# A recurrence and an MLP on one core: transposes moved to the DMA crossbar, relu and copies split over two engines, a new order of issue

## The chip, the cores and the metric

The kernel runs on one core of a Trainium2 chip. A core has a matrix engine (TensorE, PE in the profile; its weight loads are listed as PEld), two elementwise engines that can read the matrix results in PSUM (VectorE, DVE, and ScalarE, ACT), a third one that works from SBUF (GpSimd, POOL), and a queue engine (SyncE, SP) that in this kernel issues every DMA. Each engine runs its own list of instructions in order and waits on semaphores where its data or its buffer come from another. The metric is the device time of one execution in microseconds (us), median of several.

## The reference

Four sequences of 768 tokens with 8 heads of 48 columns go through a decaying recurrence, and its output through a two-layer MLP:

```python
# r, k, v, w: (4, 8, 768, 48) float32, u: (8, 48)
for t in range(S):
    cur = einsum('bhd,bhe->bhde', u[None] * kt, vt)
    y[:, :, t] = einsum('bhd,bhde->bhe', rt, state + cur)
    state = wt[:, :, :, None] * state + einsum('bhd,bhe->bhde', kt, vt)
x = y.transpose(0, 2, 1, 3).reshape(3072, 384)
h = x @ w_in                     # 384 -> 2048
g = s * relu(h) ** 2 + b
out = g @ w_out                  # 2048 -> 384, float32
```

## The kernel before

The recurrence is cut into 24 chunks of 128 tokens (the first two are packed from halves). Inside a chunk the decays become exponentials of running sums of log w, and the rest is matmuls. Two chunks make one of 12 token pairs (T), which go through the MLP. A plan names every step, and the string `ORDER` lists them in the order in which they are written to the engines' queues. `n` is a chunk, `T.i` a step of a token pair, `+18` means 18 matmuls on zeros [...], and `@A`, `@D`, `@P` move one step to ScalarE, VectorE or GpSimd.

- `load n.0 ... n.3`: w, r, k, v of a chunk, 192 KB each (384 KB where packed). `li`, `lo`: a quarter of w_in, w_out (768 KB); `ci`, `co`: its cast to bf16.
- `ln`, `cum` (TensorE: running sums, one PSUM buffer A, shared with `mt`), `exp`, from chunk 8 also `inc`, `exn`: the decay factors. `mul` (VectorE): r and k times these.
- `tr`, `tev`: r and k transposed, by TensorE and a ScalarE copy, or by one crossbar DMA (then only `tev`).
- `mt`, `msk`: scores and their mask. `ymm`, `yev`: output y, with `yd` added, the part of u (`rkp`, `rku`, `cd`, `yd`). `dmm`, `sup`, `st`: state. `vb`: cast of v.
- `xtr`, `xev`: y transposed into x for the MLP, by TensorE and a copy, or by one crossbar DMA.
- `g1` (h = x w_in, 6 matmuls, two PSUM buffers h), `relu`, `sq`, `g2` (out, 4 matmuls), `oev`, `store`.
- `colsum`, `cssplit`, `csspread`, `csevac`: the constant b times the column sums of w_out. `u_mm`, `u_ev`: u spread over 128 partitions by a matmul, and its copy to SBUF.

```python
    def xbar_rk(n):
        return n >= DTK or (n >= DK2 and n % 2 == 1)      # DTK = 9: r and k by crossbar from chunk 9
    def xbar_x(n):
        return n >= DTX or (n >= DX2 and n % 2 == 1)      # DTX = 24: x never
# ...
    def trans(n):                                          # tr: 8 matmuls
        ps = psB.tile([128, 8, 128], BF16, name="trps", tag="B")
        for x in range(2):
            for p in range(HP):
                nc.tensor.matmul(ps[:, x * HP + p, :], lhsT=c["prd"][...], rhs=identity,
                    is_transpose=True, ...)
    def dtrans(n):                                         # tev by crossbar
        RK = work.tile([128, 2 * HP, 128], BF16, name="RK", tag="RK", bufs=RKB)
        nc.sync.dma_start_transpose(out=RK, in_=c["prd"].rearrange("t x h d -> t (x h d)"))
    def dxtr(n):                                           # xev by crossbar
        nc.sync.dma_start_transpose(out=xT[T][:, :, j * L : (j + 1) * L], in_=cb[n]["x"])
    def xtr(n):                                            # 3 matmuls
        for i in range(KT):
            nc.tensor.matmul(ps[:, i, :], lhsT=c["x"][:, i * 128 : (i + 1) * 128], rhs=identity, ...)
    def xevac(n):
        nc.scalar.copy(out=xT[T][:, :, j * L : (j + 1) * L], in_=c["xt_ps"])
    def relu(T, i):
        rh = mlp.tile([128, FPQ, TOK], BF16, name="rh", tag="rh", bufs=4)
        nc.scalar.activation(out=rh, in_=hs[T, i], func=AF.Relu)
    def square(T, i):
        if pl.ops["sq", T, i]["eng"] == "ACT":
            nc.scalar.activation(out=g, in_=rh, func=AF.Square)
        else:
            nc.vector.tensor_tensor(out=g, in0=rh, in1=rh, op=ALU.mult)
# ...
    def spread_u():
        ps = psO.tile([128, HD], FP32, name="u_ps", tag="o")
        nc.tensor.matmul(ps, lhsT=one_row, rhs=u_row, start=True, stop=True)
    def u_evac():
        nc.vector.tensor_copy(out=u_bc, in_=os_.pop("u"))
```

Of the kernel before, what the change touches and what calls it, by code (L numbers as in the profile page):

```python
# [24 lines left out]
PK = 2  # L25
PKD = 1.55
ONE = 8
DTK = 9
DTX = 24
DK2 = 24  # L30
DX2 = 24
SQE = 'DA'
# [15 lines left out]
g11.3 load6.0 colsum1 rkp4 g20.1 ln5 relu1.2 tr4 rku4 relu1.3 load4.3 cum5 sq1.0@A g11.4 st1 exp5
g11.5 co2 g20.5 tev4 load5.1 sq1.3 load5.2 colsum2 sq1.1@A st3 co3 mt4 load7.0 relu1.4 g20.6
relu1.5 cd4 g11.6 load6.1 msk4 sq1.5@A colsum3 ln6 g20.7 yd4 sq1.4@A load6.2 cssplit g11.7 sq1.2@A  # L50
l25 l24 vb4@A csspread load5.3 cum6 csevac g20.2 mul5 exp6 load8.0 dmm4 g20.3 rkp5 sup4 ln7
load6.3 tr5 oev0.0 ymm4 rku5 tev5 cum7 load7.1 yev4 g21.0 oev0.1 exp7 l26 xtr4 mul6 load7.2 g21.1
xev4 mt5 relu1.6 cd5 vb5 load7.3 g21.4 relu1.7 st2 msk5 yd5 dmm5 g21.2 ln8 load9.0 sq1.7@A st4
sup5 tr6 cum8 vb6 store0.1 tev6 ymm5 rkp6 g21.5 yev5 exp8 load8.1 g21.6 inc8 l27 sq1.6@A dmm6 xtr5
mul7 g21.7 load8.3 xev5 exn8 mt6 rkp7 sup6 vb7@A load8.2 g12.0 msk6 load9.1 g12.1 rku7 ln9 tr7
oev1.1 relu2.0 load10.0 rku6 cum9 relu2.1 cd7 dmm7 g12.2 inc9 tev7 l28 load11.0 g12.3 cd6 st5
relu2.2 ymm6 yd6 sup7 load9.2 exp9 g12.4 relu2.3 sq2.0 mt7 yd7 yev6 exn9 load9.3 g12.5 relu2.4
msk7 st7 g21.3 sq2.2@A store0.0 sq2.1 rkp8 g12.6 oev1.0 sq2.3 load10.1 ymm7 relu2.6 st6 xtr6 g22.4
yev7 ln10 load10.2 mul8 relu2.5 g22.0 ln11 xtr7 sq2.4 load12.0 g22.5 xev6 sq2.6@A load10.3 cum10
vb9 g12.7 xev7 inc10 vb8 exp10 tr8 load11.1 sq2.5@D relu2.7 g22.1 l29 mul9 exn10 g13.0 load11.2  # L60
tev8 rku8 cum11 g22.6 load12.1 relu3.0 dmm9 rkp9 exp11 cd8 g13.1 sq2.7 tev9 sup9 dmm8 g13.2 rku9
relu3.1 inc11 sq3.0@A g22.2 mul10 relu3.2 load13.0 g13.3 exn11 load11.3 rkp10 sup8 mt8 relu3.3
g13.4 msk8 ln12 tev10 vb10 g22.7 sq3.2@A st9 sq3.1 g13.5 oev2.1 relu3.4 yd8 cum12 store1.0 ymm8
relu3.5 inc12 g22.3 l210 yev8 exp12 store1.1 g13.6 cd9 sq3.4@A mul11 sq3.3 xtr8 dmm10 mt9 load15.0
g23.0 yd9 msk9 vb11@A g13.7 st8 xev8 load14.0 g23.1 oev2.0 relu3.6 l212 rku10 sup10 load12.2 exn12
ymm9 g23.4 sq3.5 load12.3 yev9 relu3.7 rkp11 mt10 cd10 xtr9 tev11 g23.2 msk10 xev9 l211 rku11 ln13
g23.5 g14.0 sq3.6 load13.1 sq3.7@D cum13 load13.2 relu4.0 dmm11 g14.1 inc13 exp13 mul12 ymm10
exn13 load14.1 g14.2 ln14 l213 cd11 relu4.1 yd10 g23.6 relu4.2 cum14 sq4.0 load13.3 g14.3 exp14
yd11 sup11 g23.3 inc14 relu4.3 load16.0 st11 g14.4 sq4.1 oev3.0 st10 mt11 load14.2 yev10 relu4.4
g14.5 msk11 rkp12 sq4.2@A xtr10 load15.1 sq4.3 g14.6 vb12 ln15 g23.7 rkp13 relu4.6 load15.2 ymm11  # L70
relu4.5 cum15 yev11 rku12 g24.0 xev10 tev12 oev3.1 g14.7 ln16 mul13 xtr11 exn14 g24.4 store2.1
# [12 lines left out]
inc19 exp19 load19.1 g16.7 mul18 load19.2 g17.0 relu6.7 tev16 g26.1 exn19 ln20 dmm16 g26.5 vb18@A
sup16 load19.3 sq6.7 cum20 g17.1 vb17 inc20 relu7.0 tev17 g26.6 rkp18 sq6.6@A dmm17 relu7.1 g17.2
st16 exp20 load20.1 dmm18 g26.7 sq7.0@A mul19 exn20 g26.2 tev18 relu7.2 rkp17 oev6.1 g17.3 sup17
mt16 rku17 relu7.3 load20.2 g17.4 msk16 sq7.3 g26.3 yd16 relu7.4 load21.0 g17.5 sup18 sq7.2@A vb19
cd17 sq7.1 ymm16 rku18 tev19 oev6.0 mt17 relu7.5 g27.0 msk17 l219 yd17 g27.4 st17 load21.1 g17.6
yev16 ymm17 st18 load21.2 xtr16 mt18 yev17 xev16 g27.5 sq7.5@D relu7.6 load22.0 sq7.4 xtr17 cd18
g17.7 xev17 mul20 ln21 g27.1 relu7.7 dmm19 load20.3 yd18 msk18 g18.0 sq7.7 sq7.6@A g27.2 rkp19  # L90
store5.1 sup19 relu8.0 g27.6 rku19 mt19 tev20 g18.1 msk19 rkp21 ymm18 relu8.1 g18.2 load23.0 sq8.0
g27.3 store6.1 rku21 cd19 relu8.2 load22.1 cum21 ln22 g18.3 sq8.1@D exp21 ymm19 yd19 inc21 relu8.3
g18.4 oev7.0 sq8.2@A rkp20 g27.7 load22.2 yev19 relu8.4 yev18 g18.5 sq8.3 rku20 oev7.1 load23.1
mt20 relu8.5 load21.3 xtr18 xtr19 msk20 vb20@A g18.6 xev18 g28.0 load22.3 relu8.6 supn20 sq8.5@D
g18.7 sq8.4 xev19 store6.0 exn21 cum22 g19.0 relu8.7 inc22 rkp22 ln23 g28.1 load23.2 relu9.0 g28.4
mul21 sq8.6@A store7.0 g19.1 exp22 supn21 cd20 exn22 g28.5 tev21 yd20 relu9.1 cum23 ymm20 exp23
g19.2 yev20 g28.6 inc23 relu9.2 mul22 g19.3 sq8.7 exn23 g28.2 tev22 sq9.1 mul23 g19.4 sq9.2@A
xtr20 relu9.3 cd21 g28.3 load23.3 sq9.0 sq9.3 g28.7 yd21 oev8.0 relu9.4 store7.1 g19.5 store8.0
rku22 mt21 relu9.5 g19.6 vb22 msk21 sq9.5 st19 g29.4 vb21@A tev23 xev20 g19.7 oev8.1 relu9.6
supn22 cd22 ymm21 sq9.4@A g29.5 yd22 yev21 relu9.7 mt22 sq9.6@A vb23 g29.0 sq9.7@D xtr21 rkp23  # L100
msk22 g29.6 xev21 g29.1 rku23 g110.0 ymm22 relu10.0 g110.1 yev22 mt23 cd23 relu10.1 g110.2 yd23
msk23 xtr22 g29.7 relu10.2 supn23 sq10.0@A g110.3 xev22 ymm23 relu10.3 g110.4 yev23 g29.2 sq10.1@D
relu10.4 g110.5 sq10.3 sq10.4 oev9.1 xtr23 g110.6 relu10.5 sq10.2 xev23 g210.0 sq10.5@D relu10.6
g110.7 g111.0 relu10.7 g210.1 relu11.0 g111.1 g210.2 relu11.1 g111.2 sq11.0@A sq10.6@A g29.3
sq10.7 g111.3 oev9.0 relu11.2 g210.3 sq11.1@D relu11.3 store9.0 store8.1 g111.4 sq11.2@A g210.4
relu11.4 g111.5 g210.5 relu11.5 g111.6 sq11.5@D oev10.0 g210.6 relu11.6 sq11.3@D store10.0 g111.7
store9.1 g211.0 relu11.7 g210.7 sq11.4@A sq11.7@D sq11.6@A g211.1 oev10.1 g211.4 store10.1 g211.2
g211.8 g211.5 g211.3 g211.6 oev11.0 g211.9 g211.7 store11.0 g211.10 oev11.1 g211.11 store11.1
oev11.2 store11.2
"""  # L110

class Plan:

# [43 lines left out]
def kernel(  # L160
# [550 lines left out]
        T, j = divmod(n, CPT)  # L711
        if j == 0:
            xT[T] = mlp.tile([128, KT, TOK], BF16, name="xT", tag="xT", bufs=XTB)
        nc.scalar.copy(out=xT[T][:, :, j * L : (j + 1) * L], in_=c["xt_ps"])  # L714


    def load_win(i):
# [40 lines left out]

    def relu(T, i):
        rh = mlp.tile([128, FPQ, TOK], BF16, name="rh", tag="rh", bufs=4)  # L760
        nc.scalar.activation(out=rh, in_=hs[T, i], func=AF.Relu)  # L761
        hs[T, i] = rh

    def sq_eng(T, i):
# [385 lines left out]
```

## Time and profile before

| | |
|---|---|
| time, median of 3 (range) | 187.29 us (186.79 to 187.95) |
| profiled span | 186.2 us |
| granted TensorE clock | 0.999 |
| relu on ScalarE | 96 x 598 ns |
| square on ScalarE, on VectorE | 62 x 629 ns, 34 x 482 ns |
| x transposes: matmuls, copies | 72 x 219 ns, 24 x 478 ns |
| r and k transposes: matmuls, copies | 72 x 219 ns, 9 x 1013 ns |
| r and k transposes by crossbar | 15, landing in 3.3 us (2.7 to 5.2) |
| mask on VectorE | 24 x 1220 ns |
| bytes read, written | 25.17 MB, 4.72 MB |

A mean duration is that of one instruction from its start to its end; on TensorE and ScalarE neighbours overlap, so a sum of durations is more than the engine's busy time. In the profile PEq, SPq and DVEq are the engines' sequencers, L748 is a line of the kernel (h), L792 the out matmuls, L297 the loads, L477 the r and k transposes by TensorE, L451 and L444 `mul`, L532 the first `mt`.

### The profile page before, as it was taken

What the parts mean: (1) busy time and instruction counts of PE and PEld (TensorE: products, weight loads), DVE (VectorE), ACT (ScalarE), POOL (GpSimd) and SP (SyncE); (2) the same over time, 40 slices, a digit from 0 to 9 for tenths busy, and PEclk for the clock granted to TensorE, in tenths of its full rate; (3) what the DMA queues carried; (4) which work ended last, traced back from release to release, by engine and by line L of the source; (5) the groups of instructions that cost most, each with busy time, mean ns of one, the idle gap of its engine ahead of it and who ended that gap; (6) DMA issues with size and microseconds to landing.
All of it is one profiled execution on the core that took longest, in us unless ns stands there. A gap on an engine that the chain in (4) does not pass through costs nothing.

```text
span 186.2 us, 5073 instructions
## 1 busy us (share of the span) xinstructions
PE 180.6 (97%) x1994; PEld 142.3 (76%) x1994; DVE 131.5 (71%) x220; ACT 142.4 (76%) x277; POOL 103.8 (56%) x141
## 2 busy tenths in 40 slices
PE   7999999999999999999999999999999999999992
PEld 5667888866678788687778877877787877887871
DVE  7478888556799768986987878658788577452231
ACT  3576798797979999769798779974689886678530
POOL 3787840608798695949956265695892167100000
PEclk9999999999999999999999999999999999999999
DMA  6998999888989999999488989999698272000322
GB/s 161 264 308 239 331 318 280 295 180 177 207 190 229 197 221 240 187 213 188 118 199 171 246 164 252 194 186 208 146 212 211 59 184 59 2 0 4 112 99 86
DMA packets 117610, 34.14 MB, mean 183 GB/s; under 512 B 112338, under 2 KB 115539, under 8 KB 117587
## 3 DMA queue, kind: packets, MB, share of 16 engines
q1 hardware_dynamic: 117586, 33.83, 78.3%
q8 instruction: 15, 0.25, 0.5%
q14 instruction: 9, 0.07, 0.1%
HBM read 25.17 MB, written 4.72 MB: 160 GB/s over the span
## 4 chain that ended last, share of the span: by engine, by line
PE 74%; SPq 12%; DMA 7%; DVE 4%; issue 1%; DVEq 0%
PE o_ps L792 31%; PE h_ps L748 29%; SPq L297 8%; DMA wi_st<-in_moe_w_in_dram 5%; PE mt_ps L543 3%; DMA rkt<-in_k_dram 2%; PE y_ps L606 2%; PE xt_ps L699 2%; PE y_ps L597 2%; PE cums L388 2%; PE d_ps L638 1%; DVE gT L773 1%; SPq L719 1%; SPq L305 1%; PE trps L477 1%; SPq L729 1%
## 5 line engine op out<-in xcount | busy, mean ns | idle before, releaser
L748 PE MATMUL h_ps<-xT,w_in 128*128 128x256 bf16 x576 | 77.6, 273 | 0.1
L792 PE MATMUL o_ps<-w_out,gT 128*128 128x384 bf16 (+1 forms) x400 | 75.3, 320 | 0.0
L761 ACT ACTIVATE rh<-h_ps 128x512 bf16<-128x512 f32 x96 | 56.5, 598 | 14.5 <-PE h_ps L748 13.5
L748 PEld LDWEIGHTS <-w_in 128*128 128x128 bf16 x576 | 60.6, 114 | 6.7 <-POOL w_in L880 0.2
L792 PEld LDWEIGHTS <-gT 128*128 128x128 bf16 x400 | 36.2, 98 | 15.3
L771 ACT ACTIVATE gT<-rh 128x512 bf16<-128x512 bf16 x62 | 37.2, 629 | 0.3
L352 POOL TENSOR_TENSOR yd<-vt,cd 128x384 bf16<-128x384 f32 x22 | 20.1, 919 | 30.4 <-DVE cd L346 18.3
L554 DVE TENSOR_TENSOR mt_sb<-mt_ps,tri_strict 128x1024 bf16<-128x1024 f32 x22 | 26.8, 1219 | 4.2 <-PE mt_ps L543 3.8
L323 POOL TENSOR_TENSOR rkp<-rkt 128x384 f32<-128x384 f32 x22 | 24.5, 1112 | 4.7 <-DMA rkt<-in_k_dram 4.6
L329 POOL TENSOR_TENSOR rku<-rkp,u_bc 128x384 f32<-128x384 f32 x24 | 26.0, 1087 | 0.9
L451 DVE TENSOR_TENSOR prd<-rkt,E 128x768 bf16<-128x768 f32 x22 | 23.0, 1045 | 2.8 <-DMA rkt<-in_k_dram 1.6
L803 DVE SCALAR_TENSOR_TENSOR o_sb<-o_ps,s_bc,bconst 128x384 f32<-128x384 f32 (+1 forms) x25 | 14.9, 596 | 10.3 <-PE o_ps L792 10.0
L651 DVE TENSOR_TENSOR x_sb<-y_ps,yd 128x384 bf16<-128x384 f32 x24 | 13.2, 554 | 11.3 <-PE y_ps L606 10.4
L773 DVE TENSOR_TENSOR gT<-rh 128x512 bf16<-128x512 bf16 x34 | 15.8, 482 | 4.9 <-ACT rh L761 4.9
L714 ACT COPY xT<-xt_ps 128x384 bf16<-128x384 bf16 x24 | 11.5, 478 | 6.8 <-PE xt_ps L699 6.8
L346 DVE TENSOR_REDUCE cd<-rku 128x8 f32<-128x384 f32 x24 | 13.0, 543 | 0.9 <-POOL rku L329 0.9
L688 POOL TENSOR_TENSOR st<-stmp,l 128x384 bf16<-128x384 bf16 x16 | 13.1, 829 | 0.7 <-DVE stmp L679 0.7
L1109 PE MATMUL warm_ps<-warm_sb 128*128 128x256 bf16 x74 | 12.2, 309 | 1.1 <-DVE warm_sb L1066 1.1
L424 DVE TENSOR_TENSOR inc<-cums,logw 128x384 f32<-128x384 f32 x16 | 8.9, 554 | 5.5 <-ACT rh L761 1.6
L318 ACT ACTIVATE logw<-wt 128x384 bf16<-128x384 f32 x22 | 11.5, 522 | 1.5 <-DMA wt<-in_w_dram 1.3
L880 POOL CAST vb<-vt 128x384 bf16<-128x384 f32 x14 | 7.4, 536 | 7.6 <-DMA vt<-in_v_dram 4.9
L464 POOL TENSOR_TENSOR l<-E,par 128x8 f32<-128x8 f32 x20 | 7.0, 353 | 6.6 <-ACT E L419 4.7
(96 smaller groups left out, 198.1 us busy)
## 6 DMA issues: line engine op xcount, KB each, us to landing
out_dram<-o_sb SPq DMA_DIRECT2D x23, 192.0 KB, 2.8
wt<-in_w_dram SPq DMA_DIRECT2D x22, 192.0 KB, 3.9
rkt<-in_r_dram SPq DMA_DIRECT2D x22, 192.0 KB, 4.0
rkt<-in_k_dram SPq DMA_DIRECT2D x22, 192.0 KB, 3.8
vt<-in_v_dram SPq DMA_DIRECT2D x22, 192.0 KB, 3.7
wi_st<-in_moe_w_in_dram SPq DMA_DIRECT2D x4, 768.0 KB, 7.5
wo_st<-in_moe_w_out_dram SPq DMA_DIRECT2D x4, 768.0 KB, 7.6
pkt<-in_w_dram SPq DMA_DIRECT2D x1, 384.0 KB, 3.3
```

What stands on the lines that cost most here:

```text
L297: nc.sync.dma_start(out=dst, in_=src[bb, :, t0 : t0 + L, :].transpose([1, 0, 2]))
L323: nc.gpsimd.tensor_tensor(out=rkp, in0=c["r"], in1=c["k"], op=ALU.mult)
L329: nc.gpsimd.tensor_tensor(out=rku.rearrange("t h d -> t (h d)"), in0=c["rkp"].rearrange("t h d -> t (h d)"), in1=u_bc, op=ALU.mult,)
L352: nc.gpsimd.tensor_tensor(out=yd, in0=c["v"], in1=c["cd"].unsqueeze(2).to_broadcast([128, H, D]), op=ALU.mult,)
L451: nc.vector.tensor_tensor(out=prd[:, :, :, 0:D], in0=c["rk"], in1=c["E"][:, :, 0:HD].rearrange("t x (h d) -> t x h d", h=H), op=ALU.mult,)
L554: nc.vector.tensor_tensor(out=m.rearrange("s g p t -> s (g p) t"), in0=c["mt_ps"].rearrange("s g p t -> s (g p) t"), in1=(masks[n % 2] if ...
L748: nc.tensor.matmul(ps[:, f, :], lhsT=w_in_sb[ft // FPP][:, kt, :].rearrange("p (m j) -> p j m", j=FPP)[:, ft % FPP, :], rhs=xT[T][:, kt, : ...
L761: nc.scalar.activation(out=rh, in_=hs[T, i], func=AF.Relu)
L771: nc.scalar.activation(out=g, in_=rh, func=AF.Square)
L773: nc.vector.tensor_tensor(out=g, in0=rh, in1=rh, op=ALU.mult)
L792: nc.tensor.matmul(os_[T, k][:, cols], lhsT=gT[T][:, ft, tt * 128 : (tt + 1) * 128], rhs=w_out_sb[ft // FPP][:, ft % FPP, cols], start=(ft ...
L803: nc.vector.scalar_tensor_tensor(out=o_sb[:, cols], in0=os_.pop((T, k))[:, cols], scalar=s_bc, in1=bconst[:, cols], op0=ALU.mult, op1=ALU.add,
```

## The change

Chunk 8's r and k join those transposed by the crossbar, and so does x of the last four chunks, 20 to 23: this takes transposes from TensorE and their copies from ScalarE. `relu` and `xev`, until now always on ScalarE, may now be put on VectorE, step by step; the marks in the order say which. The order itself comes from a further search (annealing) under random delays, meant to give an order that holds when steps take longer or shorter than planned. The matmul that spreads u is issued behind the second running sum instead of ahead of it, where it is out of the first chunk's way. The diff, with the order cut to its opening and its end:

```diff
-DTK = 9
-DTX = 24
+DTK = 8
+DTX = 20
 DK2 = 24
 DX2 = 24
 ...
-load0.0 load0.1 load_u load0.2 load2.0 ln0 ln1 load2.1 +18 cum0 load2.2 u_mm exp0 load0.3 +2 cum1
-l20 mul0 li0 exp1 rkp1 u_ev +1 tr0 load3.1 ln2 mul1 tev0 load3.2 +6 cum2 rku1 +2 tr1 exp2 load2.3
-l21 tev1 mul2 vb0@A l22 cd1 +14 mt0 rkp2 vb1@A msk0 +5 dmm0 load3.0 rkp0 tr2 sup0 +1 mt1 tev2 li1
-rku0 st0 msk1 ci0 load3.3 rku2 cd0 +13 mt2 li2 ymm0 yd0 msk2 vb2@A yd1 +1 ymm1 li3 yev0 rkp3 ln3
-xtr0 yev1 xev0 +3 cum3 cd2 rku3 dmm2 xtr1 exp3 load4.0 sup2 +6 dmm1 xev1 mul3 lo0 ci1@A +2 ymm2
-g10.0 l23 cd3 yd2 sup1 g10.1 relu0.0 vb3 yev2 tr3 relu0.1 small2 yd3 g10.2 tev3 dmm3 ci2@D g10.3
-relu0.2 xtr2 sup3 mt3 sq0.0@A load4.1 g10.4 sq0.1 relu0.3 msk3 ci3 g10.5 relu0.4 lo1 xev2 ymm3 ln4
-sq0.2 relu0.5 g10.6 sq0.3 load4.2 yev3 cum4 relu0.6 load5.0 xtr3 g10.7 co0 xev3 lo2 g11.0 relu0.7
-sq0.4 sq0.5 g20.0 relu1.0 sq0.6 sq0.7 colsum0 exp4 lo3 g11.1 g11.2 co1 relu1.1 small g20.4 mul4
-g11.3 load6.0 colsum1 rkp4 g20.1 ln5 relu1.2 tr4 rku4 relu1.3 load4.3 cum5 sq1.0@A g11.4 st1 exp5
-g11.5 co2 g20.5 tev4 load5.1 sq1.3 load5.2 colsum2 sq1.1@A st3 co3 mt4 load7.0 relu1.4 g20.6
-...
-g110.7 g111.0 relu10.7 g210.1 relu11.0 g111.1 g210.2 relu11.1 g111.2 sq11.0@A sq10.6@A g29.3
-...
-store9.1 g211.0 relu11.7 g210.7 sq11.4@A sq11.7@D sq11.6@A g211.1 oev10.1 g211.4 store10.1 g211.2
-g211.8 g211.5 g211.3 g211.6 oev11.0 g211.9 g211.7 store11.0 g211.10 oev11.1 g211.11 store11.1
-oev11.2 store11.2
+load0.0 load_u load0.1 load0.2 load2.0 load2.1 ln0 ln1 load2.2 +18 cum0 exp0 load0.3 cum1 u_mm
+l20 mul0 load3.0 exp1 rkp0 u_ev +1 tr0 load3.1 ln2 mul1 tev0 load3.2 +6 cum2 l21 +2 tr1 rku0 exp2
+li0 tev1 mul2 load3.3 vb1@A l22 cd0 +14 mt0 rkp2 vb0@A tr2 msk0 ln3 load2.3 +1 dmm0 rku2 tev2 sup0
++5 mt1 li1 rkp1 st0 dmm1 msk1 rku1 sup1 +10 cum3 lo0 yd0 ymm0 cd1 exp3 yd1 +1 ymm1 load4.0 ci0
+yev0 rkp3 xtr0 li2 yev1 xev0 l23 mul3 +6 xtr1 mt2 xev1 vb2@A cd2 +3 tr3 msk2 g10.0 rku3 li3 tev3
+g10.1 st1 vb3@A cd3 dmm2 relu0.1 sup2 dmm3 ci1 mt3 small2 sq0.1@A sup3 ymm2 relu0.0@D load4.1 msk3
+yd2 g10.2 ln4 g10.3 yd3 yev2 co0@A ymm3 sq0.0 cum4 load4.2 relu0.3 g20.4 ci2@D relu0.2 exp4 sq0.3
+g10.4 yev3 load5.0 sq0.2@A g10.5 lo1 relu0.4 ci3 xtr2 xtr3 g20.0 lo2 xev2@D relu0.5@D xev3 colsum0
+lo3 g10.6 sq0.4 sq0.5@A mul4 g10.7 load4.3 relu0.6 rkp4 g11.0 relu0.7 ln5 g11.1 relu1.0 sq0.6
+load5.1 tr4 rku4 relu1.1@D g11.2 co1 cum5 relu1.2 g11.3 sq0.7@A load6.0 colsum1 exp5 g20.5 co2
+g20.1 relu1.3 cd4 sq1.3@A g11.4 small sq1.1 tev4 colsum2 sq1.0 g11.5 co3 load5.2 relu1.4 mt4
+...
+g19.6 supn22 cd22 load23.3 oev8.0 sq9.5 yd22 ymm21 relu9.6 mt22 yev21 rkp23 g29.5 msk22 xev21
+g29.0 rku23 g19.7 store7.1 g29.1 cd23 relu9.7 g29.6 sq9.6@A sq9.7 mt23 ymm22 g29.7 yd23 yev22
+g29.2 msk23 st19 xev22 g110.0 g110.1 relu10.0 g29.3 vb23@A relu10.1@D sq10.0@A g110.2 supn23
+sq10.1@D oev9.1 ymm23 relu10.2 g110.3 yev23 g110.4 relu10.3@D xev23 g210.0 oev9.0 relu10.4 g110.5
+sq10.3@D sq10.2@A store8.1 g210.4 store8.0 relu10.5@D g110.6 g210.1 relu10.6@D g110.7 sq10.5@D
+sq10.4 g210.5 relu10.7@D g111.0 sq10.7@D g111.1 relu11.0@D g210.2 sq10.6 relu11.1 sq11.0 g111.2
+...
+store9.1 g111.5 sq11.3@D sq11.2 g111.6 relu11.5 sq11.4 g211.0 sq11.5@D relu11.6@D g111.7 g211.1
+relu11.7@D g210.7 sq11.7 g211.2 sq11.6@A oev10.1 g211.4 g211.3 g211.5 oev11.0 g211.8 g211.6
+store11.0 g211.9 store10.1 g211.7 g211.10 oev11.1 g211.11 store11.1 oev11.2 store11.2
 ...
     def xevac(n):
-        nc.scalar.copy(out=xT[T][:, :, j * L : (j + 1) * L], in_=c["xt_ps"])
+        out = xT[T][:, :, j * L : (j + 1) * L]
+        if pl.ops["xev", n]["eng"] == "ACT":
+            nc.scalar.copy(out=out, in_=c["xt_ps"])
+        else:
+            nc.vector.tensor_copy(out=out, in_=c["xt_ps"])
 ...
     def relu(T, i):
         rh = mlp.tile([128, FPQ, TOK], BF16, name="rh", tag="rh", bufs=4)
-        nc.scalar.activation(out=rh, in_=hs[T, i], func=AF.Relu)
+        if pl.ops["relu", T, i]["eng"] == "ACT":
+            nc.scalar.activation(out=rh, in_=hs[T, i], func=AF.Relu)
+        else:
+            nc.vector.tensor_scalar_max(out=rh, in0=hs[T, i], scalar1=0.0)
```

Over the whole order, 29 relus and 6 `xev` carry the mark of VectorE. Squares on VectorE go from 34 to 26, V casts on ScalarE from 10 to 14, and the matmuls on zeros from 74 to 67.

## The prediction

> **What bounds the kernel now.** I read the page's busy times and slices first, then stretches of the span, then the chain in order of time, then the opening as a timeline. The page's busy line and three rows of its 40 slices:
>
> ```profile
> PE 180.6 (97%) x1994; PEld 142.3 (76%) x1994; DVE 131.5 (71%) x220; ACT 142.4 (76%) x277; POOL 103.8 (56%) x141
> PE   7999999999999999999999999999999999999992
> PEclk9999999999999999999999999999999999999999
> DMA  6998999888989999999488989999698272000322
> ```
>
> TensorE looks full all along, at full clock, and the DMA engines are nearly full for three quarters of the span. The busy share does not say whether TensorE does useful work. The stretches (columns: stretch, length, busy us of PE, PEld, DVE, ACT, POOL, then clock, DMA share, GB/s) and, below them, the warm-up tile alone in its only stretch:
>
> ```profile
> 0.00:22.00 22.00, 20.77 (x283) 14.88 (x284) 16.10 (x37) 13.38 (x23) 15.59 (x32) 1.00 0.94 254
> 50.00:160.00 110.00, 110.00 (x1201) 87.26 (x1198) 86.05 (x134) 91.47 (x186) 74.47 (x93) 1.00 0.87 183
> 160.00:182.00 22.00, 22.00 (x196) 18.03 (x191) 7.95 (x17) 13.50 (x25) 0.83 (x1) 1.00 0.13 46
> ...
> 0.00:22.00 22.00, 12.15 (x74) 1.00 0.94 254
> ```
>
> More than half of TensorE's busy time in the first 22 us is warm-up matmuls on zeros. The chain in order of time (start, length, what) tells the rest:
>
> ```profile
> 34.62 4.61 SPq L297
> 39.27 4.35 DMA rkt<-in_k_dram
> 43.74 0.97 DVE prd L451
> 44.76 0.62 PE trps L477 x8
> ...
> 171.46 0.65 PE o_ps L792 x4
> 172.11 0.65 PE h_ps L748 x6
> ...
> 176.68 5.90 PE o_ps L792 x52
> 182.60 0.42 DVE o_sb L803
> ```
>
> From 44.76 to 182.6 the chain is TensorE alone, in pieces of 0.65 us for six h matmuls (0.109 each) or four o matmuls (0.1625 each). So I add up TensorE's work at start-to-start distances: 96 h groups at 0.655 = 62.9; 92 whole o groups at 0.65 and 8 half ones at 0.33 = 62.4; 24 mt at 0.33 = 7.9; y 9.5; cums 8.1; trps 9 x 0.45 = 4.1; xt 24 x 0.167 = 4.0; d 3.7; u, column sums and their spread 2.4. With rounding 165.3 us. From the end of the last matmul (182.4) to the end of the span are 3.8 us. Then 186.2 - 165.3 - 3.8 = 17.1 us is waste: start, warm-ups (74 x 0.109 = 8.1) and waits. Subtracting the work ahead of a marker from its time places it: 12.9 us lie before the first h matmul (21.95), 0.5 more by token pair 1's first h (29.73), 1.2 more by chunk 5's trps at 44.76, which that chain shows waiting for k, and only 2.5 in the 138 us after.
>
> [...] 20.77 busy us of the first 22 hold 9.1 of work. [...] the trace's masks agree (1219 ns for 1024, 554 for 384 in the y sum, so 1.04 ns an element). [...] here a 256 KB R/K transpose lands in 3.3 us, a 192 KB load in 3.7 to 4.0.
>
> **The change, part by part.**
>
> *R and K of chunk 8 by crossbar.* Removes 8 trps matmuls, 0.45 us of TensorE, and a 1.01 us ScalarE copy. It adds one 256 KB transfer, 1.0 to 1.6 us of the DMA engines, as such transfers' packets took around 120 us. New data has landed by 143 there and is used until 160, so that is hidden.
>
> *x of the last four chunks by crossbar.* Removes 12 xt matmuls, 4 x 0.167 = 0.67 us, and four ScalarE copies of 0.48. After 155 us the DMA engines idle. The order leaves six to seven groups of 0.65 (over 4.5 us) between each pair's last y and its first h; a y sum (0.55) and a landing of about 3 fit. TensorE's work falls by 0.45 + 0.67 = 1.1 to 164.2 us.
>
> *Two-engine copies and the new order.* By its marks, 29 relus and 6 xT copies go to VectorE, squares on VectorE fall from 34 to 26, ScalarE gets 8 more squares and 4 more V casts. A relu of 512 from PSUM is 554 + 128 x 1.04 = 0.69 us, my estimate. VectorE: +29 x 0.69 + 6 x 0.5 - 8 x 0.48 - one weight cast 0.96 = +18 us, 150 in all. ScalarE: -29 x 0.6 - 10 x 0.48 - 1.0 + 8 x 0.63 + 4 x 0.5 = -16, 126 in all. Neither was the bound; ScalarE's relief gives TensorE nothing it was waiting for, and VectorE, at about 95% in token pairs 0 to 6 by such counts, becomes the tighter one.
>
> *The opening.* These lines carry it:
>
> ```profile
> 6.01 0.91 PE L901 MATMUL u_ps<-u_row,one_row 1*128 1x384 f32 x2
> 7.91 0.54 DVE L905 COPY u_bc<-u_ps 128x384 f32<-128x384 f32 x1
> 9.05 1.76 DVE L444 TENSOR_TENSOR prd<-pkt,E 128x384 bf16<-128x384 f32 x2 [0.60 <-ACT E L412]
> 12.72 0.42 PE L532 MATMUL mt_ps<-RK 48*64 48x128 bf16 x16
> 21.95 1.48 PE L748 MATMUL h_ps<-xT,w_in 128*128 128x256 bf16 x12
> ```
>
> The second sum has always waited for the first exp (one PSUM buffer A; exp ends 6.99, the sum starts 7.08), so u's 0.83 us was free there. Put behind, it ends at 8.8, its copy at 9.5, and the second product, behind the copy on VectorE, starts at 9.5 instead of 9.05. From there: product to 11.2, trps 11.8, then 14 warm-ups end at 13.25, so mt0 comes 0.5 late; mask to 14.95, second mask to 16.8 (before 16.53), the fourth sum waits for buffer A and then y0 starts at 17.5 instead of 17.03. But exp of chunk 3 is done early, so ScalarE takes the two xT copies right after the weight cast, to 21.1, and the first h comes at 21.6: 0.35 earlier, with 0.1 less work done. Warm-ups are 67 for 74 but fill waits, so I count nothing for them again. Then relu 0.0 stands on VectorE behind two state updates (end 25.0) and holds an h buffer: the third h group waits about 0.7, later ones 0.9. At pair 1's first h the waste is 14.2, against 13.4.
>
> *The weights.* Now the first w_out piece goes ahead of two w_in pieces, and k of chunk 4 and w of chunk 5 ahead of the other three w_out pieces. Counting loads in issue order at the trace's 0.93 us a 192 KB load, 2.2 a w_in piece and 2.4 a w_out piece, k of chunk 5 lands some 2 us before the 43.6 of the chain, and w_out's last piece at 36.8. Chunk 5's trps then comes when TensorE gets to it, 44.0, waste 14.2 against 14.6: 0.4 gained.
>
> *Sum.* 186.2 - 1.1 - 0.4 = 184.7 us of span; I add 0.3 for a tighter VectorE in the middle: 185.0. The timed median stands 1.1 above the profiled span (187.29 against 186.2), hence 186.1; I round to 186.0.
>
> **Rivals.** *VectorE becomes the bound.* For it: 95% in an in-order queue, and each late relu holds one of two h buffers. Against it: before ran VectorE at 0.9 for whole stretches (9.1 of 10 us at 50 to 60) and TensorE missed nothing. It would cost 2 to 4 us: 188 to 190. *The opening gains more.* If li0's landing and the copies fit better than my hand chain has them, up to the seven warm-ups and the 0.9 us of h waits come back: 184. *The tail stalls on crossbar latency*: for it, transposes took up to 5.2 us under load; against it, the DMA is idle then. One to two us: 187 to 188. *A transfer that was hidden anyway*: the last relus on two engines could speed nothing, as TensorE has no gap at 160 to 182; I believe this one and have counted nothing.
>
> **Range and chances.** The sure part is 1.1 us, or 0.6%. All waste outside the opening is 2.5 us and cannot vanish, so 2% (below 183.5) needs the opening to give 2.5 us, which my chain doesn't find: 0.07. Slower by 2% (over 191.0) needs a new bound: 0.04. Range 184.0 to 188.6, longer above than below, as a reordered program has more ways to wait than to gain.
>
> **What would show it.** trps 64 instead of 72, xt 60 for 72, TensorE alone on the chain from about 44; relu on VectorE near 0.65 to 0.69 us; the first h at 21.6; mt0 about 13.2; chunk 5's trps at 44 without a wait for k. I am wrong if TensorE waits after 50 us for a VectorE relu or an xT or RK transfer, or if the first h moves by more than a microsecond.

## The result and the profile after

The changed kernel is slower: 190.06 us median (189.72 to 190.43) against 187.56 of the kernel before, a ratio of 1.0139 with a 95% interval from 1.0099 to 1.0179. The profiled span grew from 186.2 to 188.3 us. (The ratios here leave disturbed runs out, so they are not exactly the quotient of two medians.)

The busy line of the page of the changed kernel:

```profile
PE 179.6 (95%) x1967; PEld 141.2 (75%) x1967; DVE 151.4 (80%) x246; ACT 129.3 (69%) x249; POOL 104.8 (56%) x138
```

VectorE has 20 us more (18 were predicted) and ScalarE 13 us less (16). The opening and the middle of the changed kernel as stretches (same columns as in the prediction):

```profile
0.00:22.00 22.00, 19.62 (x265) 14.08 (x266) 14.96 (x35) 13.14 (x22) 15.76 (x33) 1.00 0.90 233
50.00:160.00 110.00, 109.40 (x1175) 86.43 (x1173) 96.86 (x145) 86.17 (x174) 74.03 (x92) 1.00 0.95 187
```

In the first 22 us the DMA engines moved 233 GB/s instead of 254, and TensorE was busy for 19.62 us instead of 20.77, of which 11.03 instead of 12.15 are warm-ups. Between 50 and 160 TensorE was busy all the time before, and now for 109.40 us. From 160 to 182 it is as full as it was.

The chain in order of time (start, length, what) shows what TensorE stood behind in the opening of the changed kernel:

```profile
20.22 9.50 DMA wi_st<-in_moe_w_in_dram
...
29.78 1.47 POOL w_in L887
...
31.87 8.16 DMA wo_st<-in_moe_w_out_dram
...
40.05 0.97 DVE w_out L889
...
41.07 0.45 PE cs_ps L838 x12
```

Where the chain of before held the load of k for chunk 5, this one holds the weights: the last piece of w_in, then the last piece of w_out. From 41.07 on it is TensorE, but not for good, as it was before. Late in the span VectorE is back on it, from 144.2 to 151.6; the last part of that stretch:

```profile
147.72 1.50 DVE prd L451
...
149.82 1.13 DVE mt_sb L554
150.95 0.61 DVE rh L768
151.60 0.81 PE h_ps L752 x6
```

To compare kernels whose orders differ I use the measure of the prediction throughout: the time at which a marker on TensorE starts, less the work that this kernel's order has ahead of it. That is its waste so far, in us. One profile places such a marker to within half a microsecond to one (figures in the last section), so single differences below that are not secured. Markers: the first h group; pair 0's fifth h group; pair 1's first; chunk 5's trps; then the first h of pairs 2 and 9; and the last h groups of pair 11.

| | before | after |
|---|---|---|
| first h | 12.88 | 13.36 |
| pair 0, fifth h | 12.99 | 14.72 |
| pair 1, first h | 13.34 | 14.95 |
| chunk 5's trps | 14.61 | 16.00 |
| pair 2, first h | 14.65 | 16.57 |
| pair 9, first h | 16.71 | 19.18 |
| pair 11, last h | 17.11 | 19.91 |
| start of the last matmul to the end | 3.9 | 4.3 |

Waste at the last h rises by 2.8 and the tail by 0.4; 1.1 us of TensorE's work are gone. That is the +2.1 of the span. Two thirds of it (1.9 us) have accrued by pair 2's first h, at 55 us.

### The profile page after: what moved, and what is told of

Read it like the earlier page. It is cut to its first block, busy times and chain, and to the rows that moved or that the text cites. A ratio compares the mean times of both kernels' runs of the same rounds, so it can differ in the third digit from the quotient of the medians.

```text
span 188.3 us, 5013 instructions
## 1 busy us (share of the span) xinstructions
PE 179.6 (95%) x1967; PEld 141.2 (75%) x1967; DVE 151.4 (80%) x246; ACT 129.3 (69%) x249; POOL 104.8 (56%) x138
## 4 chain that ended last, share of the span: by engine, by line
PE 74%; DVE 10%; DMA 9%; ACT 2%; issue 2%; POOL 1%; SPq 0%; DVEq 0%; ACTq 0%
PE o_ps L799 28%; PE h_ps L752 26%; DMA wi_st<-in_moe_w_in_dram 5%; DMA wo_st<-in_moe_w_out_dram 4%; PE warm_ps L1116 4%; PE mt_ps L543 3%; DVE prd L451 3%; PE y_ps L606 2%; PE y_ps L597 2%; PE xt_ps L699 1%; PE cums L388 1%; PE d_ps L638 1%; DVE rh L768 1%; DVE mt_sb L554 1%; DVE inc L424 1%
## 5 line engine op out<-in xcount | busy, mean ns | idle before, releaser
L766 ACT ACTIVATE rh<-h_ps 128x512 bf16<-128x512 f32 x67 | 39.3, 596 | 19.7 <-PE h_ps L752 18.6
L778 ACT ACTIVATE gT<-rh 128x512 bf16<-128x512 bf16 x70 | 42.2, 629 | 5.4 <-DVE rh L768 5.1
L352 POOL TENSOR_TENSOR yd<-vt,cd 128x384 bf16<-128x384 f32 x22 | 19.1, 871 | 23.3 <-DVE cd L346 16.8
L451 DVE TENSOR_TENSOR prd<-rkt,E 128x768 bf16<-128x768 f32 x22 | 27.5, 1250 | 3.8 <-ACT E L434 2.1
L329 POOL TENSOR_TENSOR rku<-rkp,u_bc 128x384 f32<-128x384 f32 x24 | 27.4, 1145 | 1.4 <-DVE u_bc L912 0.4
L554 DVE TENSOR_TENSOR mt_sb<-mt_ps,tri_strict 128x1024 bf16<-128x1024 f32 x22 | 26.7, 1214 | 1.4 <-PE mt_ps L543 1.4
L768 DVE TENSOR_SCALAR rh<-h_ps 128x512 bf16<-128x512 f32 x29 | 19.8, 683 | 4.0 <-PE h_ps L752 2.8
L688 POOL TENSOR_TENSOR st<-stmp,l 128x384 bf16<-128x384 bf16 x16 | 15.3, 958 | 2.3 <-DVE stmp L679 2.3
L780 DVE TENSOR_TENSOR gT<-rh 128x512 bf16<-128x512 bf16 x26 | 13.3, 528 | 0.6 <-ACT rh L766 0.5
L419 ACT ACTIVATE E<-cums 128x388 f32<-128x388 f32 (+1 forms) x16 | 7.9, 494 | 7.4 <-DVE inc L424 5.4
L1116 PE MATMUL warm_ps<-warm_sb 128*128 128x256 bf16 x67 | 11.0, 312 | 1.1 <-DVE warm_sb L1073 1.1
```

Source lines behind the costliest of these rows:

```text
L329: nc.gpsimd.tensor_tensor(out=rku.rearrange("t h d -> t (h d)"), in0=c["rkp"].rearrange("t h d -> t (h d)"), in1=u_bc, op=ALU.mult,)
L352: nc.gpsimd.tensor_tensor(out=yd, in0=c["v"], in1=c["cd"].unsqueeze(2).to_broadcast([128, H, D]), op=ALU.mult,)
L451: nc.vector.tensor_tensor(out=prd[:, :, :, 0:D], in0=c["rk"], in1=c["E"][:, :, 0:HD].rearrange("t x (h d) -> t x h d", h=H), op=ALU.mult,)
L554: nc.vector.tensor_tensor(out=m.rearrange("s g p t -> s (g p) t"), in0=c["mt_ps"].rearrange("s g p t -> s (g p) t"), in1=(masks[n % 2] if ...
L688: nc.gpsimd.tensor_tensor(out=c["st_new"], in0=c["stmp"].rearrange("q p (g e) -> q p g e", g=2), in1=c["l2"].unsqueeze(3).to_broadcast([12 ...
L768: nc.vector.tensor_scalar_max(out=rh, in0=hs[T, i], scalar1=0.0)
```

## The experiments

Theory: the opening, everything ahead of pair 2's first h (`g12.0`), costs about 2 us, and the rest of the change roughly nothing. Rivals: the relus on VectorE make it the bound; u behind the second sum costs it; the crossbar stalls something. Thirteen kernels were run, one of them twice; all are below. The diffs show the words of the order that move.

**The crossbar alone, on the kernel before.**

```diff
-DTK = 9
-DTX = 24
+DTK = 8
+DTX = 20
-... tr8 ... xtr20 ... xtr21 ... xtr22 ... xtr23 ...
```

> The kernel before with one part of the change alone: r and k of chunk 8 and x of the last four chunks by crossbar, in before's order and with before's engines. Theory (the opening and the order are what cost): TensorE's work falls by 1.1 us and nothing waits for the crossbar, so the time is 1.0 us below before, 0.5 to 1.5. Rival (the crossbar transfers are what made the change slow, by their landing or by holding up the queue of loads): no gain, or 0.5 to 2 us above before.

Measured: 187.05 us, ratio 0.9974 (0.9949 to 1.0). Waste at the last h is 17.61, 0.5 more than before, so half of the 1.1 us of work taken off comes through; where the other half goes is not shown. The same kernel once more:

> The same kernel as the crossbar alone on before, run again in more rounds: the earlier ratio was 0.9974 with an interval from 0.9949 to 1.0. Theory (the transposes taken off TensorE are worth about half of their 1.1 us once the reordering is left out): 0.3 to 0.6 us faster than before, interval below 1. Rival (no gain at all): interval around 1, within 0.2 us of before.

Measured: 187.06 us, ratio 0.9968 (0.9936 to 1.0). Two estimates of 0.3% agree, and both intervals end at 1: a gain of about 0.5 us that is likely and not secured. The trace has no wait of TensorE behind 44 us, so the crossbar stalls nothing. This is also the best form that was found.

**The opening of before in the changed kernel.** All operations ahead of `g12.0` in the order and with the marks of before; the order of the change behind it. (Nine steps, such as `vb7`, `load9.3` and `msk6`, stand ahead of `g12.0` in one order and behind it in the other. In both splices they stay on the side where the kernel that is edited has them.)

```diff
-load0.0 load_u load0.1 load0.2 load2.0 load2.1 ln0 ln1 load2.2 +18 cum0 exp0 load0.3 cum1 u_mm
+load0.0 load0.1 load_u load0.2 load2.0 ln0 ln1 load2.1 +18 cum0 load2.2 u_mm exp0 load0.3 +2 cum1
 ... (all up to g12.0)
```

> The changed kernel with before's order and engine marks for all steps ahead of the first h of token pair 2, and everything behind it as changed. Theory (the opening is at fault, which holds 1.9 of the 2.8 us more waste that the trace of the changed kernel shows): 1.9 us faster than the changed kernel, so 0.5 to 1 us above before. Rival (VectorE, now 80% busy, holds TensorE up in the long middle): within 0.5 us of the changed kernel, 2.5 us above before.

Measured: 188.13 us, ratio 1.0021 (0.9997 to 1.0045). That takes 1.9 us back from 190.06. Waste at pair 2's first h is 14.66, as before (14.65).

**The opening of the change on the kernel before**, the same splice the other way round.

```diff
-... the order of before ahead of g12.0
+... the order of after ahead of g12.0
```

> The opposite splice: the changed opening, ahead of the first h of token pair 2, and behind it before's order, engines and TensorE transposes. Theory (the opening is at fault): 1.9 us above before. Rival (VectorE in the middle is at fault): no more than 0.5 us above before.

Measured: 190.21 us, ratio 1.0114 (1.0025 to 1.0203). Waste at pair 2's first h is 16.88. The two splices agree: the lateness travels with the opening. From one kernel to the next, the way from 187.56 to 190.06 is -0.5 for the crossbar, +1.1 (188.13 less 187.05) for the order and the division of work behind `g12.0`, and +1.9 for the opening. Such steps add up by construction. What bears out the 1.9 is the reverse splice, which by its ratio loses 2.1 us (0.5 to 3.8). So the gain of the transposes is eaten a first time by the rest of the change, and the opening is the loss on top.

**Relus and xT copies back on ScalarE**, in the changed kernel and, in a second form, behind `g12.0` of the kernel with the opening of before.

```diff
-... relu0.0@D ... xev2@D ... relu0.5@D ... relu1.1@D ...
+... relu0.0 ... xev2 ... relu0.5 ... relu1.1 ...
```

> The changed kernel with every relu and every copy of x back on ScalarE, in the same order. Theory (the order was made for two engines, and ScalarE has 16 us more to do there than in the changed kernel): no gain, 0 to 3 us slower than the changed kernel. Rival (relu on VectorE is the cost as such, by its 683 ns and by waiting behind VectorE's other work): 1 to 2 us faster than the changed kernel.

Measured: 190.5 us, ratio 1.0152 (1.0083 to 1.022), waste at pair 2's first h 16.30. Its four executions (190.14 to 190.81) overlap those of the changed kernel (189.72 to 190.43).

> The changed kernel with the opening of before (188.13 us), and behind g12.0 all 24 relus and four xT copies that it put on VectorE back on ScalarE; the order of every engine stays. Theory (VectorE is what TensorE waits for between 135 and 152 us, and 24 x 0.68 + 4 x 0.35 = 17.7 us less of its work behind g12.0 sets it free): waste from g12.0 to the last h down from 3.6 to about 2.6 us, time 187.0 to 187.5. Rival (the order, annealed with these operations on VectorE, is what costs; on ScalarE, which then has 126 + 24 x 0.6 us of work, the same relus come as late): waste behind g12.0 3.4 or more, time 188.0 or above.

Measured: 188.52 us, ratio 1.0051 (1.0028 to 1.0073). Waste from pair 2's first h to the last h is 3.87, and was 3.60 with the relus on VectorE. Neither form is faster, although the second takes VectorE from 94.99 to 87.04 busy us between 50 and 160. Undoing the division of work under this order gains nothing; an order made for one engine was not tried. The chain of the second form in order of time, where TensorE comes off it, shows why no engine has to be full for this:

```profile
137.63 0.54 DVE cd L344
138.17 0.48 DVE inc L422
...
138.69 0.40 PE mt_ps L541 x8
```

VectorE's list has a product (from 135.60), a square, `cd` and the sum of a later chunk (`inc`) one behind the other, and TensorE's list has an `mt` that waits for the last, which reads the PSUM buffer that `mt` writes. Fewer relus on VectorE leave that sequence as it is. The stretch of VectorE from 142.6 to 149.9 that the chain has with the relus still there is gone from this one, and the waste is no less.

**u behind the second sum, on the kernel before**, and **ahead of it in the changed kernel.**

```diff
-load2.2 u_mm exp0 load0.3 +2 cum1 l20
+load2.2 exp0 load0.3 +2 cum1 u_mm l20
```

> The kernel before with u's matmul moved behind the second sum and nothing else. Theory (the half microsecond that it adds ahead of the first scores is swallowed further on, because before's TensorE waits for k of chunk 5 at 44.8 us in any case): within 0.3 us of before, although the first scores start 0.5 us later. Rival (a delay on the first chain is carried to the end): 0.5 us above before.

Measured: 188.34 us, ratio 1.0002 (0.997 to 1.0034). The interval holds the rival's 0.5 us too, so the time does not decide. The trace speaks for the theory: the first h comes 1.07 us later (waste 13.95), and chunk 5's trps at 14.73 against 14.61. Part of what is lost early is absorbed where TensorE of before waits 0.40 us for the last piece of w_out and 0.21 for the product of chunk 5; here it comes late enough to wait for neither. Not every execution gets off so lightly: in five of the 20 the granted clock was 0.988 to 0.990, and they took 188.8 to 189.8 us (more on this in the last section).

> The changed kernel with u's matmul ahead of the second sum again. Theory (swallowed by the wait for the loads): within 0.3 us of the changed kernel. Rival (carried to the end): 0.5 us faster than the changed kernel.

Measured: 189.66 us, ratio 1.0093 (1.0067 to 1.0119). The first h comes 0.66 us earlier, and by the medians 0.4 us of the time come back, but the intervals of the two ratios overlap. The gap is plain in TensorE's timeline of the changed kernel (start, length, what, and in brackets the idle time ahead and what ended it):

```profile
7.13 0.32 PE L373 MATMUL cums<-logw,hi_pos 128*128 128x384 bf16 x1 [0.96 <-ACT E L414]
```

u's 0.91 us filled this idle time before; now it starts at 8.16, behind the second sum, where it is in the way.

**Loads against engines.** The opening consists of an order of loads and an order of the compute engines. Each can be had without the other. The loads from the seventh on, to chunk 5's k (the rest up to `g12.0` is cut):

```diff
-load2.2 load0.3 li0 load3.1 load3.2 load2.3 load3.0 li1 load3.3 li2 li3 load4.0 lo0 small2 load4.1
-lo1 load4.2 load5.0 lo2 lo3 small load6.0 load4.3 load5.1 load5.2
+load2.2 load0.3 load3.0 load3.1 load3.2 li0 load3.3 load2.3 li1 lo0 load4.0 li2 li3 small2 load4.1
+load4.2 load5.0 lo1 lo2 lo3 load4.3 load5.1 load6.0 small load5.2
```

As written, this puts the changed loads under the engine order of before (the kernel with the opening of before is what it starts from):

> The other corner: before's order and engines in the opening, only the loads there in the changed order, and everything behind the opening as changed. Theory (the loads): 1 to 1.6 us slower than with before's whole opening, so 1.5 to 2.2 us above before. Rival (the engines' order): the same as with before's whole opening within 0.4 us.

Measured: 191.4 us, ratio 1.0168 (1.0107 to 1.0228): the loads alone lose 3.3 us here, twice what the theory had. And the reverse, the loads of before under the changed engine order, first as it is and then with u ahead of the second sum as well:

> The changed kernel with one queue's order put back: the loads ahead of the first h of token pair 2 are issued in before's order; TensorE, VectorE, ScalarE and GpSimd keep the changed order. Theory (the order of the loads is what makes the opening slow: the quarters of w_in and w_out, and k of chunk 5, land 1 us and more later than before, and TensorE ends at the last of them): 1 to 1.6 us faster than the changed kernel, so 1 to 1.5 us above before. Rival (the order of the engines' work in token pair 0 and the relus on VectorE): no more than 0.4 us faster than the changed kernel.

Measured: 190.96 us, ratio 1.0172 (1.0091 to 1.0253).

> The changed kernel with both marks of its opening that can be undone without touching the order of the compute engines: the loads ahead of g12.0 in the order of before, and u ahead of the second sum again. What is left of the change is its order and division of work on TensorE, VectorE and ScalarE, and the crossbar. Theory (the order of the loads makes the lateness behind the first h, the gap that u left makes the lateness ahead of it): no wait on a load of over 0.4 us ahead of g12.0, waste at g12.0 from 16.57 to about 15.0 to 15.4, the kernel at 188.3 to 189.0 us; what then stays above before is VectorE's chain behind 135 us. Rival (the order of the compute engines in the opening is slow by itself): waste at g12.0 stays at 16 or above, time 189.6 or above, as with u ahead alone (189.66) .

Measured: 191.55 us, ratio 1.0215 (1.0147 to 1.0282). My theory for this last one, 188.3 to 189.0, was wrong by over 2 us, and the gain of 1 to 1.6 us that I expected of the loads of before alone did not come either.

| ahead of `g12.0` | loads of before | loads of after |
|---|---|---|
| engines of before | 188.13 | 191.4 |
| engines of after | 190.96 (u ahead: 191.55) | 190.06 (u ahead: 189.66) |

By the medians each mixture is slower than both pure forms. For 191.4 and 191.55 no execution overlaps those of the pure form on the same engines (188.13 and 189.66). For 190.96 against 190.06 they overlap, and in all four of its executions the granted clock had fallen (0.987 to 0.991). In the profiled one mt0 came 1.75 us late (last section), and pair 2's first h only 0.5 (55.45 against 54.93), so this corner says little of the loads. No cheap half was found. The traces of the other two say why. TensorE and VectorE with the engine order of before and the changed loads:

```profile
28.30 2.21 PE L751 MATMUL h_ps<-xT,w_in 128*128 128x256 bf16 x12 [2.31 <-DVE w_in L888]
...
27.28 0.96 DVE L888 CAST w_in<-wi_st 128x1536 bf16<-128x1536 f32 x1 [3.70 <-DMA wi_st<-in_moe_w_in_dram]
```

and TensorE and ScalarE with the changed engine order and the loads of before (u ahead):

```profile
30.63 0.81 PE L798 MATMUL o_ps<-w_out,gT 128*128 128x384 bf16 x4 [2.26 <-ACT w_out L884]
...
29.11 1.47 ACT L884 CAST w_out<-wo_st 128x1536 bf16<-128x1536 f32 x1 [1.35 <-DMA wo_st<-in_moe_w_out_dram]
```

The kernel before runs all eight h groups of pair 0 ahead of any out group and wants w_in early; the change puts an out group ahead of the fifth h group and wants a piece of w_out early. Given the other's loads, each waits over 2 us for the weight that isn't there. In the first of these traces the granted clock is 0.51 from 29.0 to 32.4, behind that wait, which adds to the loss: 12 h matmuls take 2.21 us in the line above and 1.48 at full clock. It is not all of the loss: the two executions of this kernel with a clock of 0.995 and above took 190.51 and 191.39. Order and loads had been fitted to each other.

**Mending the changed opening.** Two attempts that leave the order of the compute engines: k of chunk 5 goes out ahead of a load whose issue took 3.66 us, and then this with the w_out loads ahead of w of chunk 5 and u ahead.

```diff
-load5.1 load6.0 small load5.2 load7.0
+load5.1 load5.2 load6.0 small load7.0
```

> The changed kernel with one load moved: k of chunk 5 goes out right behind r of chunk 5, ahead of w of chunk 6, whose issue took 3.66 us, and of the small load of the second layer. Theory (the loads of the opening are issued in order and stand behind one that has to wait; this makes k of chunk 5 late by about 2 us): the wait of 1.34 us for it in VectorE's multiplication of chunk 5 goes, waste at g12.0 from 16.57 to about 15.6 to 16.1, time 189.2 to 189.7 us. Rival (TensorE comes to chunk 5's transposes no sooner, because of what is late ahead of them): the wait goes, and waste at g12.0 stays within 0.3 us of 16.57, time 189.9 to 190.3.

Measured: 191.48 us (190.16 to 193.17), ratio 1.0173 (1.0097 to 1.0248). Two of the four executions had a granted clock of 0.978 and 0.979 and took 192.6 and 193.2 us, so the median says little of the load; the profiled one took 190.37 at full clock. VectorE's product of chunk 5, in the changed kernel and with the earlier load:

```profile
44.85 0.96 DVE L451 TENSOR_TENSOR prd<-rkt,E 128x768 bf16<-128x768 f32 x1 [1.34 <-DMA rkt<-in_k_dram]
```

```profile
43.84 0.96 DVE L450 TENSOR_TENSOR prd<-rkt,E 128x768 bf16<-128x768 f32 x1 [0.23 <-DMA rkt<-in_k_dram]
```

The wait for k went, the product came a microsecond sooner, and waste at pair 2's first h is 16.80 against 16.57. The load that looks guilty in the waits of VectorE was not on TensorE's path, since TensorE itself came late: the rival held.

```diff
-load4.2 load5.0 lo1 lo2 lo3 load4.3
+load4.2 lo1 lo2 lo3 load5.0 load4.3
-cum0 exp0 load0.3 cum1 u_mm
+cum0 u_mm exp0 load0.3 cum1
```

> The changed kernel with three repairs of its opening together: k of chunk 5 sooner, the three loads of w_out ahead of w of chunk 5 (whose issue took 2.94 us), and u ahead of the second sum. The order of the compute engines stays else. Theory (late loads and the gap at u make up the lateness of the opening): no wait for w_out over 0.3 us, waste at g12.0 from 16.57 to about 14.8 to 15.3, time 188.2 to 188.8, near the changed kernel with the opening of before (188.13 and 188.52 with its rest on one engine or two). Rival (the order of the compute engines in the opening has waits of its own, between the first h and that of pair 1): waste at g12.0 15.6 or more, time 189.2 or above.

Measured: 196.35 us, ratio 1.042 (1.0352 to 1.0489). By its number that is the rival's (189.2 or above), but the cause is one that neither had. The first h comes 1.0 us earlier than in the changed kernel and no wait for the later pieces of w_out is left. But w of chunk 5, now behind them, arrives at 38.5, and ScalarE's list has its logarithm ahead of a relu. The chain of this kernel, and in its timeline the matmul that waits:

```profile
31.16 7.37 DMA wt<-in_w_dram
...
38.55 0.02 ACT logw L317
...
38.98 0.59 ACT rh L765
```

```profile
39.61 1.44 PE L751 MATMUL h_ps<-xT,w_in 128*128 128x256 bf16 x6 [5.04 <-ACT rh L765]
```

The relu needs nothing from w of chunk 5. It only stands behind it in an engine's list, and TensorE pays 5.04 us. It pays once more behind the wait, where the granted clock (third figure from the end) is halved:

```profile
40.00:45.00 5.00, 5.00 (x35) 3.10 (x34) 1.34 (x2) 3.73 (x7) 3.05 (x5) 0.50 0.98 188
```

The six h matmuls of 1.44 us above take 0.82 at full clock. My estimate from this line: these five microseconds do 2.5 us of work. All four executions of this kernel show a fallen clock (0.974 to 0.991).

**x by crossbar in the last eight chunks**, the attempt to go further with what worked.

```diff
-DTX = 20
+DTX = 16
-... xtr16 ... xtr17 ... xtr18 ... xtr19 ...
```

> The kernel before with the crossbar for R, K from 8 and x in the last eight chunks (the change has the last four), nothing else: 12 transposes of x more leave TensorE, 12 x 55.5 ns = 0.67 us. Theory (the transposes are on the path and their crossbar transfers are hidden as in the last four): 0.3 to 0.6 us under the form with the last four (187.05), 186.4 to 186.8 us, with the waste behind g12.0 at 2.9 to 3.3 us. Rival (a crossbar transfer of about 2.3 us and its wait in the queue of loads comes too late for x, whose xT is needed soon after, or holds up the loads behind it): TensorE waits for xT at g18 to g110, time 187.1 or above.

Measured: 190.41 us, ratio 1.014 (1.0072 to 1.0207). TensorE waits at the two pairs that are new on the crossbar:

```profile
133.57 0.82 PE L746 MATMUL h_ps<-xT,w_in 128*128 128x256 bf16 x6 [1.51 <-DMA xT<-x_sb]
...
146.11 0.82 PE L746 MATMUL h_ps<-xT,w_in 128*128 128x256 bf16 x6 [1.88 <-DMA xT<-x_sb]
```

The rival held. 0.67 us of work saved, 3.39 us of waits got. There the order leaves less time between y and h than in the last four chunks (1.9 us from the end of the y sum to where TensorE is free for the first of these h groups), and the DMA engines still have loads to carry: SyncE issues five between 126.9 and 134.8, around the first of the two waits, and x lands in 2.3 to 3.3 us, where the four of the changed kernel take 2.3 to 2.4.

## Why the prediction was wrong

The step that failed is the opening, above all its weights. I let the new opening give up 0.8 us of waste by pair 1's first h and win back 1.2 by chunk 5's trps: 0.4 gained. Measured, it gives up 1.6, wins back 0.2 and loses another 0.5 by pair 2's first h: the 1.9 of the splices. The rest of the change and the step from span to time were missed by less. The predicted span was 185.0, the measured one 188.3; the 3.3 us come as follows.

*The opening up to the first h* ("the first h comes at 21.6"): it came at 22.34, so the waste there is 13.36 instead of 12.6, 0.75 more, which is hardly above what one profile can tell. mt0 (predicted 13.25, measured 13.31) and the start of y0 (17.5, measured 17.8) were near. What failed is the last link: I followed the data, y to x to the copies of xT, which end at 21.51, and let h start there. In TensorE's list mt of chunk 2 and trps of chunk 3 stand ahead of that h, and the trps wait for VectorE's product. Timelines of TensorE and VectorE, changed kernel:

```profile
21.88 0.62 PE L477 MATMUL trps<-identity,prd 128*128 128x128 bf16 x8
22.34 1.47 PE L752 MATMUL h_ps<-xT,w_in 128*128 128x256 bf16 x12
...
20.49 1.33 DVE L451 TENSOR_TENSOR prd<-rkt,E 128x768 bf16<-128x768 f32 x1
```

*From the first h to pair 1's first h* I had 1.6 us (from 12.6 to 14.2: waits behind late relus); 1.59 were measured. The size was right, the reason at most in part: with every relu on ScalarE in the same order this stretch runs from 22.53 to 32.82, only 0.3 us shorter than here (22.34 to 32.94).

*The weights* ("k of chunk 5 lands some 2 us before the 43.6 of the chain, and w_out's last piece at 36.8. Chunk 5's trps then comes when TensorE gets to it, 44.0, waste 14.2"): wrong by 1.05 us beyond what it inherited. It took k for what TensorE waits for, since k was on the chain. But before, TensorE stood only 0.21 us for k's product:

```profile
44.76 0.62 PE L477 MATMUL trps<-identity,prd 128*128 128x128 bf16 x8 [0.21 <-DVE prd L451]
```

And k did not land 2 us sooner: the product started at 44.85 (before: 43.74). I counted loads at the rate at which the DMA engines move them and left out that SyncE issues in order, where one issue can take long (4.04 us for a piece of w_in from 13.51 on in the changed kernel), and waits for staging buffers: there the issue of w_out's last piece waited 1.5 us for GpSimd's cast of w_in, and the piece took 8.16 us from there to land. The cast of w_in's last piece in the timeline, first of the kernel before and then of the changed one, and below it the column sums that wait for w_out's last piece, show the lateness:

```profile
26.21 1.46 POOL L880 CAST w_in<-wi_st 128x1536 bf16<-128x1536 f32 x1 [2.10 <-DMA wi_st<-in_moe_w_in_dram]
```

```profile
29.78 1.46 POOL L887 CAST w_in<-wi_st 128x1536 bf16<-128x1536 f32 x1 [4.28 <-DMA wi_st<-in_moe_w_in_dram]
...
41.07 0.45 PE L838 MATMUL cs_ps<-ones,w_out 128*128 128x1 bf16 x12 [0.85 <-DVE w_out L889]
```

w_in is whole 3.6 us later, and w_out's last piece lands at 40.0 instead of 36.8, so that the last column sums, which stand in TensorE's list ahead of what follows, wait 0.85 of the 1.05 us (before: 0.40). That w_out's lateness costs this much is read from the trace and not shown by undoing it: the one attempt turned it into a larger wait.

*Chunk 5's trps to pair 2's first h*: 0.57 us in small gaps where before has 0.04. I had nothing for it.

*The rest* ("I add 0.3 for a tighter VectorE in the middle"): from pair 2's first h to the last h, waste grew by 3.34 against 2.46 before, 0.9 more instead of 0.3. The sign that I had named for being wrong came: at 151.60 an h on the chain starts behind a VectorE relu. The rival "VectorE becomes the bound" has the right engine on the chain, and its 188 to 190 us is close to what was measured, by luck: with 8 us less to do there VectorE frees nothing. What is left is the order in which the lists wait for each other; this was argued from the chains and not taken apart by a run. The tail gave 0.4 more.

*The sizes that came from rows* were right for TensorE, whose work fell by 1.1 us (trps 64, xt 60). VectorE is busy 151.4 (predicted 150), in part by luck, as 4.5 us of it were in no term of mine (last section). ScalarE is busy 129.3 (126), and the relu on VectorE, estimated at 0.69, is in the group list of the changed kernel with

```profile
L768 DVE TENSOR_SCALAR rh<-h_ps 128x512 bf16<-128x512 f32 x29 | 19.8, 683 | 4.0 <-PE h_ps L752 2.8
```

The last 0.7 between 186.0 and 190.06 is the step from the span to the time. I set the median of before, 187.29, against the span of an execution that had itself taken 187.99, and got 1.1. In that one execution time and span are 1.8 apart, and in the profiled one of the changed kernel 2.1 (190.43 and 188.3); its median stands 1.8 above the span.

What stays open is which decision inside the changed engine order of the opening loses the time. Loads and u were separated from it, and the division under the same order; the order was not taken apart further. Nor was it tried whether annealing under random delays helps as such, as no order annealed without them and otherwise the same is at hand.

## What to carry to other kernels

Where a search has placed every instruction of several in-order engines and of the load queue, the order is one fitted object: predict a marker by everything that stands ahead of it in its own engine's list and in the lists of those it waits for, the queue of loads with its buffers included, and not by its data path. A new order of the opening has to be worth more than its waits before half a microsecond of saved transposes counts; try the structural part of such a change alone on the old order first. And before moving a load that is waited for, ask what in the in-order lists stands behind the load that it overtakes. A wait of TensorE in the opening can cost more than its length: here one of 5.0 us was followed by a granted clock of 0.50 over the next five (the mended opening), and of two of 2.3 us one was followed by 0.51 over 3.4 us (the changed loads under the engines of before).

## What was not expected of the hardware

*VectorE's product is slower beside GpSimd.* The group of `mul` (busy us, mean ns, idle time ahead) in the changed kernel; in the one before the same 22 took 23.0 us, 1045 ns each:

```profile
L451 DVE TENSOR_TENSOR prd<-rkt,E 128x768 bf16<-128x768 f32 x22 | 27.5, 1250 | 3.8 <-ACT E L434 2.1 <-DMA rkt<-in_k_dram 1.3 <-ACT E L412 0.3
```

Laying GpSimd's spans over the single products gives 949 ns for those with no GpSimd elementwise operation beside them and 1298 on average, up to 1830, for the 19 of 22 that overlap one in the changed kernel; before, 15 of 22 overlap, with 1091 on average against 951. The masks, which read PSUM, stay the same (1219 and 1214 ns, and within the changed kernel 1215 beside GpSimd and 1210 without). Why the product takes longer there, these runs do not show. The 4.5 us that the product gains in all were in no step of mine; the 1.33 us product ahead of the first h, with 0.95 when alone, is one of them.

*TensorE's clock fell in some executions of kernels with a short idle time early on.* A stretch of the changed kernel with the loads of before; the granted clock is the third figure from the end:

```profile
10.00:13.40 3.40, 3.40 (x28) 2.57 (x26) 2.12 (x4) 1.96 (x4) 1.27 (x2) 0.51 1.10 317
```

Six matmuls on zeros take 1.46 us there and 0.82 in the profiled execution of the changed kernel, where the clock stays at 1.00; mt0 comes 1.75 us late (15.06), 0.52 of it from ahead of 7.65, where single matmuls of the first sum took 0.52 us instead of 0.32. Both executions had the same idle 0.96 us at 7 us, and only one of them had this fall. Falls are more frequent with the gap, as the mean granted clock of the single executions shows. With u behind the second sum (0.64 us idle in its profile), 5 of 20 executions of the kernel before are under 0.992 (a fall as above, 3.4 us at 0.51 in a span of 188, takes 0.009 from the mean by my estimate); with u ahead, 1 of 118. Of the changed kernel 2 of 4 are, and none of 18 with u ahead again. Where in these executions the clock fell is not shown. In the kernel before, the five took 188.8 to 189.8 us where the other 15 have a median of 187.9; the two of the changed kernel took no longer than the rest.

How long an idle time goes with a fall, the profiled executions leave open. Ahead of this one TensorE was idle for 0.96 us, ahead of the one under the loads of after (0.51) for 2.31, and ahead of that of the mended opening (0.50) for 5.04. Behind the 2.26 us under the loads of before with u ahead, 12 h matmuls took 1.47 us, the time at full clock.

*One profile can only be read so finely.* The opening of before, unchanged in four other kernels here, put the first h at 21.95, 22.53, 22.09, 22.50 and 22.02, and chunk 5's trps at 44.76, 44.83, 44.77, 43.95 and 44.86.
